# Decode kernel (grouped-query attention mixed with a gated MLP): the output row summed in two halves on two column groups, the final copy on two engines

## The chip, the cores and the metric

The kernel runs on one core of one Trainium2 chip. The metric is the device time of one execution in microseconds.

## The reference

One token is decoded. `g` is a scalar gate, `a` attention over a cache of 65,536 positions with 16 query heads and 8 key/value heads of size 256, `b` a small gated MLP, and the result is one row of 448 numbers.

```python
def reference(A_x, A_k_cache, A_v_cache, A_wq, A_wo, B_x, B_W_gate, B_W_up, B_W_down, gate_w):
    g = sigmoid((A_x * gate_w).sum(-1))
    q = (x @ wq) as 16 heads of 256
    o = softmax(q k^T / 16) v          # k, v: [8 heads, 65536, 256] bf16, 256 MiB each
    a = o @ wo                         # 4096 -> 448
    h = max(x @ W_gate, 0) * (x @ W_up)
    b = h @ W_down                     # 1792 -> 448
    return g * a + (1 - g) * b
```

## The kernel before

K and V come in tiles of 8 MiB through a ring of three buffers. Each K tile is transposed on VectorE and multiplied on TensorE; each V tile is multiplied on TensorE. The gates are folded in earlier, so that the MLP's down projection (`f_dn`) and the attention's output projection (`f_wo`) can add into one bank of PSUM (the memory that the matmul engine writes its sums to), `A_ps`. Both have a single output row: the weight operand is one column of 128 values, and the moving operand is a 128x448 block. A column group below is the part of the matmul array that `tile_position=(0, 32 * g)` selects in the code; its output row lies in PSUM partition 32 * g.

```python
# the MLP's weights live in ring buffer 2, which the third K tile will overwrite
wd_sb = ring[2][:, 0:FT * D].rearrange("p (ft d) -> p ft d", ft=FT)
slot, held, freed = {}, {2: ["gu", "dn"]}, {}      # K tile 2 waits for gate/up and for the down projection
...
def f_dn(e):                                       # 14 matmuls, one column group
    for ft in range(FT):
        ins = e.matmul(A_ps[0:1, 0:D], hT[:, ft:ft + 1], wd_sb[:, ft, :], start=(ft == 0), stop=False, ...)
...
def f_wo(e, ...):                                  # 32 matmuls, s=0 in partition 0, s=1 in partition 32
    for j in range(lo, hi):
        for s in range(2):
            r_ = 32 if s == 1 and j < J - 1 else 0     # the very last j: both in partition 0
            ins = e.matmul(A_ps[r_:r_ + 1, 0:D], attnT[:, c:c + 1], wo_sb[:, j, s, :], ..., tile_position=(0, r_))
...
if i == 3:                                         # partition 32 is copied out while the last two matmuls run
    f0 = op("ac", ..., lambda e: e.copy(a_sb, A_ps[32:33, 0:D]), ...)
f1 = op("dv", T_END, lambda e: e.tensor_tensor(fin_o, A_ps[0:1, 0:D], a_sb, ALU.add), [fin, f0])
f2 = dma("sp", T_END + 1, "out", lambda e: e.dma_start(out[0, :, :], fin_o), [f1])
```

Of the kernel before, what the change touches and what calls it, by code (L numbers as in the profile page):

```python
# [7 lines left out]
F32 = mybir.dt.float32  # L8
# [4 lines left out]
ALU = AluOpType  # L13
# [11 lines left out]
class _Plan:  # L25
# [8 lines left out]
    def op(self, eng, key, fn, deps=()):  # L34
        o = _Op(eng, key, fn, deps)
        self.ops.append(o)
        return o

    def dma(self, eng, key, sem, fn, deps=()):
        if sem not in self.dsem:  # L40
            self.dsem[sem] = self.es.enter_context(self.nc.semaphore("d_" + sem))
        o = _Op(eng, key, fn, deps, dma=sem)
        self.ops.append(o)
        return o
# [46 lines left out]
def bass_gated_mix__gqa_block_cached__glu_gated_reglu__decode_kernel(  # L91
# [13 lines left out]
    H = A_k_cache.shape[1]  # L105
    S = A_k_cache.shape[2]
    DH = A_k_cache.shape[3]
    D = A_x.shape[2]
    F = B_W_gate.shape[1]
    NQ = A_wq.shape[1]  # L110
    J = 2 * H
# [15 lines left out]
    with es:  # L127
# [5 lines left out]
        ptp = [sb("ptp%d" % i, [128, 1024], BF) for i in range(2)]  # L133
# [18 lines left out]
        attnT = sb("attnT", [128, H * 4], BF)  # L152
        hT = sb("hT", [128, FT], BF)
# [7 lines left out]
        fin_o = P_sb[0:1, 0:D]  # L161
        gw_row = ptp[1][0:1, 0:D]
        xeo = ptp[1][0:1, 448:704]
        qrep = ptp[1][:, 704:960]
        a_sb = ptp[H % 2][0:1, 0:2 * D].bitcast(F32)
        gtmp = ptp[0][0:1, 0:2 * D].bitcast(F32)

        wq3 = ring[2][:, 0:R3 * NQ]
# [6 lines left out]
        wd_sb = ring[2][:, 0:FT * D].rearrange("p (ft d) -> p ft d", ft=FT)  # L175
# [4 lines left out]
        A_ps = ps("A_ps", [128, 512], F32)  # L180
# [11 lines left out]
        op, dma = pl.op, pl.dma  # L192
# [31 lines left out]
        T_END = t + 20.0  # L224
# [9 lines left out]
        wo_sb = ring[slot["wo", 0]][:, 0:J * 2 * D].rearrange("p (j s n) -> p j s n", j=J, s=2)  # L234
# [103 lines left out]
        def f_qk(n, b, sl):  # L338
# [12 lines left out]
                return ins  # L351
            return f

        l_, qk, smax, aexp, pv, last = {}, {}, {}, {}, {}, {}
        pending = []

# [40 lines left out]
        for kind, i, t in issue:  # L397
# [34 lines left out]
            elif kind == "wd":  # L432
                a3 = dma("sp", t, "wd", lambda e: e.dma_start(wd_sb, B_W_down.rearrange("(p ft) d -> p ft d", ft=FT)), [l_["q"]])

                def f_dn(e):
                    for ft in range(FT):
                        ins = e.matmul(A_ps[0:1, 0:D], hT[:, ft:ft + 1], wd_sb[:, ft, :], start=(ft == 0), stop=False,
                                       skip_group_check=True)
                    return ins
                l_["dn"] = op("pe", max(tg + 12.2, tL["wd", 0]), f_dn, [l_["hT"], a3])  # L440
            elif kind == "k":
                n = i
# [13 lines left out]
                if t_ == NTH - 1:  # L456
# [12 lines left out]
                    ev = []  # L469
# [53 lines left out]
                l_["wo", i] = dma("sp", t, "wo%d" % i, lambda e, lo=lo, hi=hi: e.dma_start(  # L523
                    wo_sb[:, lo:hi, :, :], A_wo[lo * 256:hi * 256, :].rearrange("(j p s) n -> p j s n", p=128, s=2)), free(("wo", 0)))


        LAST = last["tn", H - 1]
        for i, (lo, hi) in enumerate(WO):
            for h in range(lo // 2, (hi + 1) // 2):
                key = max(tL["wo", i], last["tn", h] + 0.5) + 0.01 * h  # L530
                if i in (1, 2):
                    key = LAST - (0.7, 0.2)[i - 1]
                elif i > 2:
                    key = LAST + 2 + 0.1 * i

                def f_wo(e, h=h, lo=max(lo, 2 * h), hi=min(hi, 2 * h + 2)):
                    for j in range(lo, hi):
                        for s in range(2):
                            c = h * 4 + s * 2 + j - 2 * h
                            r_ = 32 if s == 1 and j < J - 1 else 0  # L540
                            ins = e.matmul(A_ps[r_:r_ + 1, 0:D], attnT[:, c:c + 1], wo_sb[:, j, s, :],  # L541
                                           start=(s == 1 and j == 0), stop=(j == J - 1 or (j == J - 2 and s == 1)),
                                           skip_group_check=True, tile_position=(0, r_))
                    return ins
                fin = op("pe", key, f_wo, [l_["wo", i], last["norm", h], l_["dn"]])
                if i == 3:
                    f0 = op("ac", key + 0.01, lambda e: e.copy(a_sb, A_ps[32:33, 0:D]), [fin, last["ev", H - 2][1]])
        f1 = op("dv", T_END, lambda e: e.tensor_tensor(fin_o, A_ps[0:1, 0:D], a_sb, ALU.add), [fin, f0])
        f2 = dma("sp", T_END + 1, "out", lambda e: e.dma_start(out[0, :, :], fin_o), [f1])

        pl.serialize(touch_m)
        progs = pl.finish()
# [53 lines left out]
```

## Time and profile before

| | before |
|---|---|
| median of the first three runs | 1284.96 us (1284.89 to 1285.78) |
| span of the profiled run | 1284.6 us |
| busy: PE, DVE, ACT | 33%, 49%, 5% |
| read from HBM | 549.03 MB, 427 GB/s over the span |

In the profiles PE is TensorE, the matmul engine, and PEld its weight loads; DVE is VectorE, ACT ScalarE, POOL GpSimd, and SPq the queue from which SyncE issues loads. These lines are from the page of the kernel before: the first gives busy time of each engine, the second the busy share of the 16 DMA engines in tenths for 40 slices of the span.

```profile
PE 425.8 (33%) x4554; PEld 159.9 (12%) x4554; DVE 633.8 (49%) x421; ACT 61.6 (5%) x116; POOL 4.1 (0%) x21
...
DMA  9999999999999999999999999999999999999997
...
DMA packets 12974, 549.65 MB, mean 428 GB/s; under 512 B 1283, under 2 KB 3590, under 8 KB 3974
```

No compute engine is near full, and the DMA row is full everywhere but in the last slice: the body waits for memory. Work on an engine can then cost time in only two ways: it can hold back the issue of a load until the DMA engines run dry, or it can lie behind the last load. Both exist here. First, part of the chain of work that ended last (start us, length us, what):

```profile
53.14 5.08 PE ST L348 x54
58.23 2.61 PE A_ps L437 x14
...
60.85 0.33 SPq L445
...
61.23 43.56 DMA ring<-in_A_k_cache_dram
```

L437 is the down projection. When its 14 matmuls are done, the SP queue issues the third K tile (L445). Second, the end of the kernel, from its timeline (start us, length us, engine, line, operation, output<-input, shape, count, and in brackets the idle time before):

```profile
1278.73 0.69 DVE L381 CAST o_sb<-O 128x512 bf16<-128x512 f32 x1 [55.80 <-PE O L370]
...
1279.21 0.91 PE L541 MATMUL A_ps<-ring,attnT 128*1 128x448 bf16 x4 [0.54 <-DMA ring<-in_A_wo_dram]
...
1280.35 2.04 PE L541 MATMUL A_ps<-ring,attnT 128*1 128x448 bf16 x8
1280.36 0.16 DVE L390 TENSOR_TENSOR attnT<-M_ps,hs 128x4 bf16<-128x4 f32 x1 [0.94 <-PE M_ps L386]
...
1281.67 0.52 ACT L547 COPY ptp<-A_ps 1x448 f32<-1x448 f32 x1 [58.86 <-PE A_ps L541]
1282.43 0.61 DVE L548 TENSOR_TENSOR P_sb<-A_ps,ptp 1x448 bf16<-1x448 f32 x1 [1.91 <-PE A_ps L541]
1283.07 0.32 SPq L549 DMA_DIRECT2D out_dram<-P_sb  x1
```

The matmuls at 1279.21 start when the last big piece of output weights has landed. From there to the output's issue it takes 1283.07 - 1279.21 = 3.86 us. I call this "the end" below; it is a chain without gaps to hide in. The last eight matmuls take 2.04 us, and one VectorE addition of 0.61 us stands alone behind them.

### The profile page before, as it was taken

How to read it: one execution, taken by the hardware profiler on the slowest of the kernel's cores; microseconds unless marked ns; L12 is line 12 of the kernel's file. 1: busy time of each engine (PE TensorE's matmuls, PEld its weight loads, DVE VectorE, ACT ScalarE, POOL GpSimd, SP SyncE). 2: the span in 40 equal slices, each digit the busy share in tenths (PEclk: the TensorE clock that was granted, in tenths of full speed). 3: DMA queues.
4: the chain of work that ended last, by engine and by line, in shares of the span. 5: the costliest groups of instructions: out<-in, count | busy, mean ns of one | idle time of the engine just before them, and what ended most of it. 6: DMA issues, size and time to landing. Idle time of an engine off the chain costs nothing.

```text
span 1284.6 us, 9827 instructions
## 1 busy us (share of the span) xinstructions
PE 425.8 (33%) x4554; PEld 159.9 (12%) x4554; DVE 633.8 (49%) x421; ACT 61.6 (5%) x116; POOL 4.1 (0%) x21
## 2 busy tenths in 40 slices
PE   3624322334123431224331343331333323233235
PEld 2401100111001110001110111110111101011011
DVE  2588633465433655434555444555434556335600
ACT  0000000000000000000000000000000000000000
POOL 1000000000000000000000000000000000000000
PEclk8656666656566565666655666655666656666676
DMA  9999999999999999999999999999999999999997
GB/s 398 420 425 447 429 429 439 431 429 435 439 427 432 430 437 435 427 437 437 429 427 437 437 427 433 433 433 429 445 429 425 435 435 431 433 435 429 437 397 315
DMA packets 12974, 549.65 MB, mean 428 GB/s; under 512 B 1283, under 2 KB 3590, under 8 KB 3974
## 3 DMA queue, kind: packets, MB, share of 16 engines
q1 hardware_dynamic: 12930, 549.03, 99.2%
q8 instruction: 35, 0.57, 0.2%
q14 instruction: 5, 0.04, 0.0%
q10 hardware_dynamic: 4, 0.00, 0.0%
HBM read 549.03 MB, written 0.00 MB: 427 GB/s over the span
## 4 chain that ended last, share of the span: by engine, by line
DVE 34%; DMA 32%; another core or an unknown queue 16%; PE 15%; SPq 1%; ACT 1%; issue 1%
DVE ring L336 30%; DMA ring<-in_A_k_cache_dram 27%; PE ST L348 7%; PE O L370 6%; DMA ring<-in_B_W_up_dram 3%; DMA ring<-in_A_wo_dram 2%; DVE P_sb L473 1%; SPq L514 1%; DVE nmb L451 1%; PE PT L478 1%; PE M_ps L421 1%; PE M_ps L424 0%; ACT ptp L487 0%; DVE o_sb L381 0%
## 5 line engine op out<-in xcount | busy, mean ns | idle before, releaser
L336 DVE STREAM_TRANSPOSE ring<-ring 128x2048 uint32<-128x2048 uint32 x256 | 565.4, 2275 | 413.1 <-DMA ring<-in_A_k_cache_dram 413.1
L348 PE MATMUL ST<-ring,xm 128*16 128x512 bf16 x2048 | 224.7, 613 | 759.0 <-DVE ring L336 759.0
L348 PEld LDWEIGHTS ST<-ring,xm 128*16 128x16 bf16 x2048 | 61.6, 120 | 908.1 <-DVE ring L336 799.4
L370 PE MATMUL O<-ring,ptp 128*4 128x512 bf16 x2048 | 146.2, 447 | 34.5 <-DMA ring<-in_A_v_cache_dram 30.4
L453 ACT ACTIVATE P_sb<-ST,nmb 128x512 bf16<-128x512 f32 x32 | 45.2, 1411 | 1115.8 <-DVE nmb L451 1115.8
L451 DVE TENSOR_REDUCE nmb<-ST 128x1 f32<-128x512 f32 x32 | 22.1, 689 | 110.4 <-PE ST L348 110.4
L370 PEld LDWEIGHTS O<-ring,ptp 128*4 128x4 bf16 x2048 | 53.9, 98 | 126.6 <-issue 54.3
L381 DVE CAST o_sb<-O 128x512 bf16<-128x512 f32 x8 | 5.5, 692 | 79.3 <-PE O L370 79.3
L473 DVE TENSOR_TENSOR P_sb<-P_sb,hs 128x1024 bf16<-128x1024 bf16 x16 | 18.9, 1222 | 8.3 <-ACT hs L467 8.3
L478 PE MATMUL PT<-identb,P_sb 128*128 128x128 bf16 x128 | 16.5, 311 | 15.5 <-DVE P_sb L473 14.7
L421 PE MATMUL M_ps<-xT,ring 128*128 128x1 bf16 x84 | 9.5, 205 | 16.3 <-DMA ring<-in_B_W_up_dram 16.3
L478 PEld LDWEIGHTS PT<-identb,P_sb 128*128 128x128 bf16 x128 | 12.3, 141 | 18.3 <-DVE P_sb L473 18.3
L487 ACT COPY ptp<-PT 128x256 bf16<-128x256 bf16 x32 | 10.3, 375 | 23.0 <-PE PT L478 23.0
L308 PE MATMUL M_ps<-ring,P_sb 128*128 128x256 bf16 x64 | 10.0, 334 | 3.2 <-DMA ring<-in_A_wq_dram 3.2
L421 PEld LDWEIGHTS M_ps<-xT,ring 128*128 128x128 bf16 x84 | 7.2, 152 | 16.9 <-issue 16.5
L453 ACT ACTIVATION_READ_ACCUMULATOR P_sb<-ST,nmb 128x1 f32 x32 | 8.4, 262 | 0.0
L308 PEld LDWEIGHTS M_ps<-ring,P_sb 128*128 128x128 bf16 x64 | 7.5, 119 | 5.5 <-issue 3.2
L424 PE MATMUL M_ps<-xT,ring 128*64 128x1 bf16 x56 | 7.8, 276 | 0.0
L404 DVE STREAM_TRANSPOSE ptp<-P_sb 128x128 uint32<-128x128 uint32 x1 | 0.3, 312 | 13.4 <-ACT P_sb L403 13.4
L463 PE MATMUL M_ps<-identf,hs 128*2 128x128 f32 x8 | 2.4, 296 | 10.0 <-DVE hs L461 10.0
L424 PEld LDWEIGHTS M_ps<-xT,ring 128*64 128x64 bf16 x56 | 5.4, 191 | 0.4
L541 PE MATMUL A_ps<-ring,attnT 128*1 128x448 bf16 x32 | 5.0, 430 | 0.6 <-DMA ring<-in_A_wo_dram 0.5
(72 smaller groups left out, 59.4 us busy)
## 6 DMA issues: line engine op xcount, KB each, us to landing
ring<-in_A_v_cache_dram SPq DMA_DIRECT2D x1, 4096.0 KB, 29.6
ring<-in_A_wq_dram SPq DMA_DIRECT2D x1, 3072.0 KB, 10.4
ring<-in_A_wo_dram SPq DMA_DIRECT2D x1, 2240.0 KB, 30.1
ring<-in_A_v_cache_dram SPq DMA_DIRECT2D x1, 2048.0 KB, 22.9
ring<-in_B_W_down_dram SPq DMA_DIRECT2D x1, 1568.0 KB, 20.7
ring<-in_B_W_gate_dram SPq DMA_DIRECT2D x1, 1344.0 KB, 32.8
ring<-in_B_W_up_dram SPq DMA_DIRECT2D x1, 1344.0 KB, 35.4
ring<-in_A_v_cache_dram SPq DMA_DIRECT2D x1, 1024.0 KB, 24.9
```

The costliest lines, as they stand in the source:

```text
L308: ins = e.matmul(QN_ps, xw3[:, k_, 31 - j:159 - j], rhs, start=(j == 0 and kt == 0), stop=(j == J - 1 and kt == R3))
L336: return lambda e: e.transpose(v, v)
L348: ins = e.matmul(bank[32 * w:32 * w + 16, :], xm[:, x0:x0 + 16], ktv[sl][:, u0:u0 + 16, c, :, r_], start=(b == 0 and c == 0 and r_ == 0), ...
L370: ins = e.matmul(OP[h % 2][32 * g:32 * g + 4, :], ptp[h % 2][:, col:col + 13:4], ring[sl][:, k * 512:(k + 1) * 512], start=(a == 0 and k < ...
L421: e.matmul(GU_ps[:, c:c + 1], wf3[which][:, kt * F + ft:(kt + 1) * F:FT], xT[:, kt:kt + 1], start=(kt == 0), stop=False, skip_group_check= ...
L424: ins = e.matmul(GU_ps[64 * half:64 * half + 64, c:c + 1], wfh[which][:, ft:F // 2:FT], xT[:, R3 + half:R3 + half + 1], start=False, stop= ...
L451: smax[n] = op("dv", tk + 22, lambda e, n=n, NM=NM, t_=t_: e.tensor_reduce(NM[:, t_:t_ + 1], ST[n % 2][:], AX.X, ALU.max, negate=True), [q ...
L453: aexp[n] = op("ac", tk + 23, lambda e, n=n, t_=t_, NM=NM, RS=RS: e.activation(P_sb[:, t_:2048:4], ST[n % 2][:], ACTF.Exp, bias=NM[:, t_:t ...
L473: rsc = op("dv", tt, lambda e, X=X, pb=pb: e.tensor_tensor(pb, pb, X[:, 12:16].unsqueeze(1).to_broadcast([128, 256, 4]), ALU.mult), [h7, a ...
L478: ins = e.transpose(PT[rd][:, s * 128:(s + 1) * 128], P_sb[:, (rd * 8 + s) * 128:(rd * 8 + s + 1) * 128], identb[:, :])
L487: ins = e.copy(dst, src)
L514: dep = dma("sp", t, "vp%d" % i, lambda e, sl=sl, n=n, lo=lo, hi=hi: e.dma_start(ring[sl][:, lo * 256:hi * 256], v_src(n)[:, lo * 256:hi * ...
```

## The change

Each projection matmul of 448 columns becomes two of 224 on two column groups (partition 0 and partition 32). The halves need no addition at the end; VectorE copies one and ScalarE the other.

```diff
+        D2 = D // 2
+        def proj(e, lhsT, rhs, start, stop):
+            for g in range(2):
+                ins = e.matmul(A_ps[32 * g:32 * g + 1, 0:D2], lhsT, rhs[:, g * D2:(g + 1) * D2], start=start, stop=stop,
+                               skip_group_check=True, tile_position=(0, 32 * g))
+            return ins
...
-                        ins = e.matmul(A_ps[0:1, 0:D], hT[:, ft:ft + 1], wd_sb[:, ft, :], start=(ft == 0), stop=False,
-                                       skip_group_check=True)
+                        ins = proj(e, hT[:, ft:ft + 1], wd_sb[:, ft, :], ft == 0, False)
...
-                            r_ = 32 if s == 1 and j < J - 1 else 0
-                            ins = e.matmul(A_ps[r_:r_ + 1, 0:D], attnT[:, c:c + 1], wo_sb[:, j, s, :],
-                                           start=(s == 1 and j == 0), stop=(j == J - 1 or (j == J - 2 and s == 1)),
-                                           skip_group_check=True, tile_position=(0, r_))
+                            ins = proj(e, attnT[:, c:c + 1], wo_sb[:, j, s, :], False, j == J - 1 and s == 1)
...
-                if i == 3:
-                    f0 = op("ac", key + 0.01, lambda e: e.copy(a_sb, A_ps[32:33, 0:D]), [fin, last["ev", H - 2][1]])
-        f1 = op("dv", T_END, lambda e: e.tensor_tensor(fin_o, A_ps[0:1, 0:D], a_sb, ALU.add), [fin, f0])
-        f2 = dma("sp", T_END + 1, "out", lambda e: e.dma_start(out[0, :, :], fin_o), [f1])
+        f0 = op("dv", T_END, lambda e: e.tensor_copy(fin_o[:, 0:D2], A_ps[0:1, 0:D2]), [fin])
+        f1 = op("ac", T_END, lambda e: e.copy(fin_o[:, D2:D], A_ps[32:33, 0:D2]), [fin])
+        f2 = dma("sp", T_END + 1, "out", lambda e: e.dma_start(out[0, :, :], fin_o), [f0, f1])
```

More of the change, by code (lines that the diff above doesn't have):

```diff
@@ L164, in bass_gated_mix__gqa_block_cached__glu_gated_reglu__decode_kernel @@
         qrep = ptp[1][:, 704:960]
-        a_sb = ptp[H % 2][0:1, 0:2 * D].bitcast(F32)
         gtmp = ptp[0][0:1, 0:2 * D].bitcast(F32)
```

## The prediction

> **What bounds the kernel now.** The page shows 549.65 MB moved at 428 GB/s, the DMA row in its top tenth in every slice but the last. The Trainium skill, "DMA: Bandwidth & Descriptors", section "Where 436 GB/s comes from", gives a fabric ceiling of 435 GB/s[...]. PE is busy 33%, DVE 49%, ACT 5%. So the body is bound by the stream from HBM; engine time counts only where it delays a load's issue while the queue runs dry, and behind the last load.
>
> **What the change touches.** Only 46 matmuls of 448 columns (14 in the down projection, L437, and 32 in the output projection, L541) and the last two copies. Each matmul becomes two of 224 columns on two column groups.
>
> **1. Down projection, on the issue path of a K tile.** The waits of the SP queue show one K load waiting 37.5 us for L437, and the chain of waits shows L437 at 58.23 us for 2.61 us, then the K issue at 60.85. The 14 matmuls run one after another in one column group, 0.19 us apart at full clock. The packet records show that around 61 to 63 us about 12 of 16 DMA engines stand empty, on average 0.66 us per engine, before the packets of this load start. As 14 pairs of 224 columns on two groups, the work should need about 14 x 0.09 us = 1.3 to 1.6 us (estimate; the score matmuls of L348 run at 53 ns each on four groups, so issuing keeps up). The K load is then issued about 1.1 us earlier and the gap mostly closes. A few engines did not idle there, so I count 0.3 to 0.7 us of it, say 0.4.
>
> **2. Output projection, behind the last load.** The first 20 matmuls (1258.6 us) lie under loads. The last 12 run at half clock (windows view: 0.50). They were already paired on two groups, except the last two, which run one after the other. The final eight take 2.04 us: five steps of about 0.37 us. After: eight steps of about 0.19 us, so about 0.35 us less. If issuing twice as many pairs binds, only 0.1 us. The Trainium skill, "TensorEngine Tiling (Array Packing)", section "Key Properties", says tiles load weights and multiply in parallel; L370's 64 matmuls on four groups agree (83 ns each where one shows 447 ns).
>
> **3. Final copy.** The DVE addition of 1x448 takes 0.612 us at the very end; the ACT copy (0.523 us) was hidden. Now DVE and ACT each copy 224 elements in parallel: estimate 0.38 us DVE (128x512 cast took 0.69), 0.36 us ACT. Saves 0.2 us.
>
> **Sum.** 0.4 + 0.3 + 0.2 = 0.9 us, 0.07% of the time. Predicted 1284.0 us; range 1281.8 to 1285.8. Chances: faster by over 2%: 0.01; within 2%: 0.98; slower by over 2%: 0.01.
>
> **What would show each step.** (1) L437's group: 28 matmuls, span near 1.4 us; the K issue near 59.8 us; the empty stretch near 61 us smaller. (2) 64 matmuls in the output projection; from the last attention scaling on DVE to the final copy about 1.5 us instead of 1.9. (3) Two copies of about 0.37 us side by side. DMA volume and rate unchanged.
>
> **What would make it wrong.** The DMA engines that never idled set the pace, so step 1 gives nothing; the halves serialize in one group (down projection stays 2.6 us); a switch of tile layout between the transposes and the projection costs more than before; or runs differ by more than the effect (three runs before spread 0.9 us).

## The result, and the profile after

The changed kernel took 1285.04 us (median of four runs, 1284.70 to 1285.65), beside 1285.37 us for the kernel before (four runs, 1284.89 to 1286.22). The ratio is 0.9997, with a 95% interval of 0.998 to 1.0015. By these runs alone nothing can be told apart from zero.

The traces say more. The same part of the chain in the changed kernel, where the down projection is L358:

```profile
52.92 5.17 PE ST L347 x54
58.09 1.34 PE A_ps L358 x27
...
59.44 0.33 SPq L452
...
59.81 43.62 DMA ring<-in_A_k_cache_dram
```

The down projection went from 2.61 to 1.34 us in the chain, and the K tile was issued at 59.44 instead of 60.85 us. The end, from the timeline of the changed kernel:

```profile
1277.46 0.69 DVE L389 CAST o_sb<-O 128x512 bf16<-128x512 f32 x1 [57.09 <-PE O L378]
...
1278.50 0.91 PE L358 MATMUL A_ps<-ring,attnT 128*1 128x224 bf16 x8 [1.08 <-DMA ring<-in_A_wo_dram]
...
1279.61 1.66 PE L358 MATMUL A_ps<-ring,attnT 128*1 128x224 bf16 x16
1279.64 0.16 DVE L398 TENSOR_TENSOR attnT<-M_ps,hs 128x4 bf16<-128x4 f32 x1 [1.48 <-PE M_ps L394]
...
1281.31 0.34 ACT L550 CAST P_sb<-A_ps 1x224 bf16<-1x224 f32 x1 [61.04 <-PE A_ps L358]
1281.31 0.38 DVE L549 CAST P_sb<-A_ps 1x224 bf16<-1x224 f32 x1 [1.51 <-PE A_ps L358]
1281.73 0.32 SPq L551 DMA_DIRECT2D out_dram<-P_sb  x1
```

The end now takes 1281.73 - 1278.50 = 3.23 us, 0.63 less: the last matmuls 1.66 instead of 2.04 us (sixteen halves in eight steps, where there were five whole steps), and the last copy 0.38 instead of 0.61 us. The page of the changed kernel shows the same stream: 428 GB/s and a full DMA row. The profiled spans differ by 1.3 us (1284.6 and 1283.3), almost four times what the means of the runs differ by (0.35 us). Part of this is the draw: the profiled execution of the kernel before took 1286.37 us, longer than all of its four timed runs. So the question was which number is the change's, and what makes the other.

### The profile page after: what moved, and what is told of

Its sections match the earlier page's. It is cut to its first block, busy times and chain, and to the rows that moved or that the text cites. A ratio compares the mean times of both kernels' runs of the same rounds, so it can differ in the third digit from the quotient of the medians.

```text
span 1283.3 us, 9919 instructions
## 1 busy us (share of the span) xinstructions
PE 427.0 (33%) x4600; PEld 162.9 (13%) x4600; DVE 633.6 (49%) x421; ACT 61.5 (5%) x116; POOL 4.1 (0%) x21
## 4 chain that ended last, share of the span: by engine, by line
DVE 34%; DMA 32%; another core or an unknown queue 16%; PE 15%; SPq 1%; ACT 1%; issue 1%
DVE ring L335 30%; DMA ring<-in_A_k_cache_dram 27%; PE ST L347 7%; PE O L378 6%; DMA ring<-in_B_W_up_dram 3%; DMA ring<-in_A_wo_dram 2%; DVE P_sb L480 1%; SPq L521 1%; DVE nmb L458 1%; PE PT L485 1%; PE M_ps L429 1%; PE M_ps L432 0%; ACT ptp L494 0%; DVE o_sb L389 0%
## 5 line engine op out<-in xcount | busy, mean ns | idle before, releaser
L378 PE MATMUL O<-ring,ptp 128*4 128x512 bf16 x2048 | 149.0, 453 | 34.3 <-DMA ring<-in_A_v_cache_dram 30.3
L358 PE MATMUL A_ps<-ring,attnT 128*1 128x224 bf16 x64 | 4.6, 305 | 2.5 <-DMA ring<-in_A_wo_dram 2.5
```

The lines of the kernel that those rows point to most:

```text
L378: ins = e.matmul(OP[h % 2][32 * g:32 * g + 4, :], ptp[h % 2][:, col:col + 13:4], ring[sl][:, k * 512:(k + 1) * 512], start=(a == 0 and k < ...
```

## The experiments

My theory: the change saves at two places, by an earlier K issue (because the DMA engines run dry before it) and by a shorter end. Rival A: an earlier K issue gives nothing, because a few DMA engines never idled there. Rival B: the gain is given back elsewhere.

Each experiment was timed in rounds beside the kernel before on the same chip. The table gives mean times; the difference is to the mean of before (nine runs each, means of 1285.99 to 1286.23 us). r1 to r4 share nine runs of before, r5 to r8 another, r9 to r11 a third; r12 has its own.

| run | what | runs | mean us | less than before | lowest to highest |
|---|---|---|---|---|---|
| r1_after_again | the change | 5 | 1285.04 | 1.15 | 1284.69 to 1285.64 |
| r2_dn_pair | down projection only | 5 | 1285.70 | 0.49 | 1284.46 to 1286.43 |
| r3_tail_only | end only | 5 | 1285.67 | 0.52 | 1284.98 to 1286.47 |
| r4_early_dn | before, down projection earlier in order | 5 | 1285.48 | 0.71 | 1284.16 to 1286.35 |
| r5_before_dn5 | before, down projection five times | 4 | 1296.87 | -10.85 | 1296.65 to 1297.33 |
| r6_after_dn5 | the change, down projection five times | 4 | 1289.97 | -3.95 | 1289.14 to 1290.43 |
| r7_one_copier | the change, VectorE copies both halves | 5 | 1284.74 | 1.28 | 1283.86 to 1285.59 |
| r8_four | four column groups | 5 | 1285.29 | 0.73 | 1284.28 to 1286.37 |
| r9_split_before | before, K load cut in two | 5 | 1284.07 | 1.92 | 1283.82 to 1284.37 |
| r10_split_after | the change, K load cut in two | 5 | 1283.30 | 2.69 | 1283.23 to 1283.34 |
| r11_split_four | four groups, K load cut in two | 5 | 1283.81 | 2.17 | 1283.47 to 1284.04 |
| r12_split_one | r10, VectorE copies both halves | 5 | 1283.94 | 2.29 | 1283.58 to 1284.38 |

The second table is from the traces, one per run. "Lost" is worked out from the DMA packet records between 58 and 75 us: the time that engines stood without a packet (counted as the packets in flight that were missing to 16) plus the time by which 64 KB packets took longer than their usual 2.42 us, both summed and divided by 16 engines. "Weights landed" is the start of the first projection matmuls of the end, which wait for the output weights. Where the load was cut, "K tile issued" is its first piece.

| trace | matmul clock rises, us | down projection starts, us | its matmuls take, us | K tile issued, us | lost, us | weights landed, us | the end, us |
|---|---|---|---|---|---|---|---|
| before | 55.90 | 58.02 | 2.81 | 60.85 | 1.56 | 1279.21 | 3.86 |
| after | 55.77 | 57.89 | 1.51 | 59.44 | 0.63 | 1278.50 | 3.23 |
| r1_after_again | 58.13 | 59.18 | 1.50 | 60.72 | 1.48 | 1278.72 | 3.27 |
| r2_dn_pair | 57.56 | 58.85 | 1.49 | 60.38 | 1.64 | 1278.24 | 3.85 |
| r3_tail_only | 55.62 | 57.74 | 2.46 | 60.23 | 0.89 | 1278.45 | 3.22 |
| r4_early_dn | 58.38 | 56.09 (weights) | about 4.2 | 60.28 | 1.27 | 1277.74 | 3.84 |
| r5_before_dn5 | 57.87 | 58.94 | 13.40 | 72.38 | 12.43 | 1289.49 | 3.85 |
| r6_after_dn5 | 57.16 | 58.43 | 6.88 | 65.34 | 5.50 | 1282.56 | 3.27 |
| r7_one_copier | 55.45 | 57.68 | 1.55 | 59.26 | 0.06 | 1276.86 | 3.66 |
| r8_four | 57.03 | 58.56 | 0.90 | 59.49 | 0.97 | 1277.42 | 2.98 |
| r9_split_before | 57.20 | 58.78 | 2.81 | 53.33 | 0.04 | 1276.52 | 3.84 |
| r10_split_after | 56.22 | 58.09 | 1.54 | 53.00 | 0.04 | 1276.75 | 3.26 |
| r11_split_four | 58.02 | 58.98 | 0.86 | 53.08 | 0.04 | 1277.07 | 2.98 |
| r12_split_one | 56.24 | 58.13 | 1.52 | 53.04 | 0.04 | 1277.03 | 3.65 |

### r1_after_again: the change once more

No edit.

> The changed kernel once more, with more rounds. My theory (0.4 us from the earlier K issue, 0.6 us from the shorter end) expects 0.6 to 1.2 us less than before, a ratio near 0.9993. Rival A (the earlier K issue gives nothing, since a few DMA engines never idled) expects 0.4 to 0.6 us less. Rival B (all of it is given back, as the end of the stream moves by more than that) expects 0 +- 0.2 us. In the trace: end of the last projection matmul group to the end of the final copy as in the first profile (final copy 0.38 us).

It was 1.15 us faster than before (ratio 0.999, interval 0.9976 to 1.0004), within what my theory expected but not clear of zero. Its trace holds the surprise: the same kernel as in the first profile issued the K tile 1.28 us later, at 60.72 us, nearly as late as the kernel before. The score matmuls and the K issue, from the timeline of the first trace of the changed kernel:

```profile
52.85 5.24 PE L347 MATMUL ST<-ring,xm 128*16 128x512 bf16 x64
...
59.44 0.80 SPq L452 DMA_DIRECT2D ring<-in_A_k_cache_dram  x2
```

The same in r1_after_again:

```profile
53.25 6.11 PE L347 MATMUL ST<-ring,xm 128*16 128x512 bf16 x64
...
60.72 0.80 SPq L452 DMA_DIRECT2D ring<-in_A_k_cache_dram  x2
```

These are the busy times by microsecond in the first trace of the changed kernel (window, its length, busy us and count of PE, PEld, DVE, ACT, POOL, granted matmul clock, DMA share, GB/s):

```profile
55.00:56.00 1.00, 1.00 (x16) 0.32 (x12) 0.00 (x0) 0.00 (x0) 0.00 (x0) 0.62 0.15 66
56.00:57.00 1.00, 1.00 (x24) 0.47 (x20) 0.00 (x0) 0.00 (x0) 0.00 (x0) 1.00 1.88 803
57.00:58.00 1.00, 1.00 (x24) 0.48 (x18) 0.00 (x0) 0.00 (x0) 0.00 (x0) 1.00 0.63 262
```

And these are the same windows in r1_after_again:

```profile
55.00:56.00 1.00, 1.00 (x16) 0.34 (x12) 0.00 (x0) 0.00 (x0) 0.00 (x0) 0.50 0.15 66
...
57.00:58.00 1.00, 1.00 (x16) 0.36 (x12) 0.00 (x0) 0.00 (x0) 0.00 (x0) 0.50 0.64 262
58.00:59.00 1.00, 1.00 (x24) 0.41 (x18) 0.00 (x0) 0.00 (x0) 0.00 (x0) 0.94 1.12 467
```

In the first trace the matmul clock went from half to full speed within the microsecond from 55 us, in the second only in the one from 58 us. The score matmuls ahead of the down projection end 1.27 us later: they started 0.40 us later, and at the slower clock they took 0.87 us longer. The Trainium skill, "TensorE: Matmul & The Clock Gate", section "What's actually happening", says that the clock is set by a free-running activity window of 3413 ns, so that the moment of the change depends on where the window happens to lie. The traces agree with the window: the clock records change at distances of 3.41, 6.83, 10.24 us and so on, all whole multiples of 3.41. For the size of the variation the section gives ±500 ns; here the rise falls anywhere between 55.45 and 58.38 us (second table), 2.65 to 5.24 us after the score matmuls began, and this measured range decides. The one-column matmuls before them did not raise the clock: from 40 to 50 us in the trace of before PE was busy for all 10 us, at half clock. So the K issue carries a delay that differs from run to run by about as much as the change saves there.

### r2_dn_pair: only the down projection on two groups

```diff
-                        ins = e.matmul(A_ps[0:1, 0:D], hT[:, ft:ft + 1], wd_sb[:, ft, :], start=(ft == 0), stop=False, ...)
+                        r_ = 32 * (ft % 2)
+                        ins = e.matmul(A_ps[r_:r_ + 1, 0:D], hT[:, ft:ft + 1], wd_sb[:, ft, :], start=(ft < 2), stop=False,
+                                       ..., tile_position=(0, r_))
```

> The kernel before with only the down projection spread over two column groups: even terms in one, odd terms in the other, still 448 columns each, the end unchanged. My theory: the 14 matmuls take about 1.4 us instead of 2.6, the K issue after them comes 1.1 to 1.4 us earlier, and the whole is 0.3 to 0.7 us faster than before. Rival A: the K issue is earlier too, but the time is unchanged (within 0.2 us).

The 14 matmuls took 1.49 us instead of 2.81, so what helps is that two groups work at once, whether each gets half of the columns or half of the terms. The run was 0.49 us faster on average (interval of the ratio 0.9983 to 1.0008), in line with the theory but, with runs 2 us apart, not proof. What was left out of the diff: `f_wo` no longer starts the sum of partition 32, which the down projection now does. In its one trace the clock rose at 57.56 us, and the K issue was only 0.47 us earlier than in the trace of before.

### r3_tail_only: the halves of the down projection one group after the other

```diff
-                    for ft in range(FT):
-                        ins = proj(e, hT[:, ft:ft + 1], wd_sb[:, ft, :], ft == 0, False)
+                    for g in range(2):
+                        for ft in range(FT):
+                            ins = e.matmul(A_ps[32 * g:32 * g + 1, 0:D2], hT[:, ft:ft + 1],
+                                           wd_sb[:, ft, g * D2:(g + 1) * D2], start=(ft == 0), stop=False, ...)
```

> The changed kernel with the halves of the down projection issued one column group after the other: 14 matmuls of 224 columns in the first, then 14 in the second. My theory: they no longer overlap, so the 28 take about 2.6 us (14 x 2 x 0.093) or more, the K issue is back near 60.8 us, and only the end is shorter: 0.5 to 0.7 us faster than before by the trace of the end. Rival: if halving the width alone were what helps, the 28 would take about 1.5 us.

The 28 halves took 2.46 us in this order and 1.51 us interleaved. Narrower matmuls alone save little (2.81 to 2.46 us); the order that keeps both groups busy saves the rest. The run was 0.52 us faster than before on average (interval of the ratio 0.9983 to 1.0008), and its end took 3.22 us, as in the changed kernel.

### r4_early_dn: the down projection moved ahead

```diff
-                l_["relu"] = mop("dv", tg + 12, ...)
+                l_["relu"] = mop("dv", tg + 8, ...)
-                l_["hT"] = mop("dv", tg + 12.1, ...)
+                l_["hT"] = mop("dv", tg + 8.1, ...)
-                l_["dn"] = op("pe", max(tg + 12.2, tL["wd", 0]), f_dn, [l_["hT"], a3])
+                l_["dn"] = op("pe", tg + 8.2, f_dn, [l_["hT"], a3])
```

> The kernel before with nothing but the order changed on the matmul engine: the down projection goes between the two halves of the first tile's score matmuls rather than behind them. The K issue that waits for it should come near 57.3 us, 3.5 us earlier, so the empty stretch of the DMA engines near 61 us vanishes altogether. My theory: 0.5 to 0.7 us faster than before, all of the 0.66 us gap. Rival A (engines that never idled set the pace): unchanged within 0.2 us. A cost could come back: the second half of the scores is 2.6 us later.

This missed. The projection did start about 2 us earlier, at 56.09 us, but there it ran at half clock, and the K issue came at 60.28 us, not 57.3. These are weight loads of it and the K issue, from the timeline:

```profile
56.52 0.12 PEld L437 LDWEIGHTS A_ps<-ring,hT 128*1 128x1 bf16 x1 [0.30 <-issue]
56.89 0.13 PEld L437 LDWEIGHTS A_ps<-ring,hT 128*1 128x1 bf16 x1 [0.24 <-issue]
57.26 0.13 PEld L437 LDWEIGHTS A_ps<-ring,hT 128*1 128x1 bf16 x1 [0.24 <-issue]
...
60.28 2.10 SPq L445 DMA_DIRECT2D ring<-in_A_k_cache_dram  x2
```

They come 0.37 us apart, twice the 0.19 us of the full clock. The move put the serial matmuls into the cold stretch; a reordering that is right by count can be wrong by clock. The 0.71 us by which its runs were faster (interval of the ratio 0.9981 to 1.0006) can't be told from zero.

### r5_before_dn5 and r6_after_dn5: the down projection five times

```diff
-                    for ft in range(FT):
+                    for ft in list(range(FT)) * 5:
```

> The kernel before with the down projection done five times over (each pass starts the sum anew, so the result stays right). The K issue comes 4 x 2.61 = 10.4 us later. My theory: the queue is empty by then, so nearly every microsecond is paid: 9 to 10.5 us slower than before. Rival A (other engines or later slack absorb a late K issue): under 5 us slower.

> The changed kernel with the down projection done five times over. Each pass of 28 half-width matmuls on two groups costs about 1.3 us, so the K issue comes 5.2 to 5.6 us later than in the changed kernel. My theory: 4 to 5.6 us slower than before, so 5 us less than the same fivefold in the kernel before. If the halves did not overlap, both fivefold kernels would be equally slow.

Here the effect is far above the noise: the intervals of both ratios (1.0084, from 1.007 to 1.0098, and 1.003, from 1.0017 to 1.0044) lie clear of 1. Four added passes cost the kernel before 10.85 us, 2.71 each; a pass of it is 14 x 0.19 = 2.6 us long. Four passes cost the changed kernel 3.95 + 1.15 = 5.1 us (taking r1, on another chip, as its time without them), 1.3 each. The two timelines show the passes (140 and 70 matmuls) and the K issue. First the kernel before with five passes:

```profile
58.94 13.40 PE L437 MATMUL A_ps<-ring,hT 128*1 128x448 bf16 x70
...
72.38 0.80 SPq L445 DMA_DIRECT2D ring<-in_A_k_cache_dram  x2
```

Then the changed kernel with five passes:

```profile
58.43 6.88 PE L358 MATMUL A_ps<-ring,hT 128*1 128x224 bf16 x140
...
65.34 0.80 SPq L452 DMA_DIRECT2D ring<-in_A_k_cache_dram  x2
```

From one to the other the K issue moved by 7.04 us and the landing of the weights at the far end by 6.93 us (1289.49 - 1282.56). A late K issue is paid one for one, 1200 us later: Rival A falls, at least where the queue has run dry. The Trainium skill, "TensorEngine Tiling (Array Packing)", section "Key Properties", says that different tiles load weights and multiply in parallel; here 140 half-width matmuls took 6.88 us and 70 full ones 13.40 us, which agrees.

### r7_one_copier: ScalarE left out

```diff
-        f1 = op("ac", T_END, lambda e: e.copy(fin_o[:, D2:D], A_ps[32:33, 0:D2]), [fin])
+        f1 = op("dv", T_END + 0.01, lambda e: e.tensor_copy(fin_o[:, D2:D], A_ps[32:33, 0:D2]), [fin])
```

> The changed kernel with both final copies on VectorE, one after the other, ScalarE left out. The second copy starts after the first: about 0.38 us more at the end of the chain, so between the last matmul and the output's issue 0.8 us instead of 0.42. The time should be 0.3 to 0.5 us above the changed kernel's. Rival: waiting for one engine rather than two makes up for it, difference under 0.1 us.

By time it came out level with the change or better, on another chip than r1 (1.28 us below before, where the change was 1.15 below), against my expectation. By its trace the end took 3.66 us, 0.4 us more than with two copiers, exactly as expected; but the clock rose early (55.45 us), nothing was lost at the K issue (0.06 us), and the weights landed 1.6 us earlier than in the first trace of the changed kernel. The trace is of the fastest of the five runs. The part that differs from run to run was larger than the effect and can have hidden it. This is why the kernels r9 to r11 were made.

### r8_four: four column groups

```diff
-            for g in range(2):
-                ins = e.matmul(A_ps[32 * g:32 * g + 1, 0:D2], lhsT, rhs[:, g * D2:(g + 1) * D2], ...)
+            for g in range(4):
+                ins = e.matmul(A_ps[32 * g:32 * g + 1, 0:D4], lhsT, rhs[:, g * D4:(g + 1) * D4], ...)
...
+        f0 = op("dv", T_END, lambda e: e.tensor_copy(fin_o, A_ps[:, 0:D4]), [fin])       # 128 x 112
+        f2 = dma("sp", T_END + 1, "out", lambda e: e.dma_start(out[0, 0, :].rearrange("(g n) -> g n", g=4), fin_o[0:128:32, :]), [f0])
```

`A_ps` is also cleared at the start, since all its partitions are copied.

> The change taken one step on: four column groups of 112 columns, one VectorE copy of 128 partitions by 112 for all of them, output written from partitions 0, 32, 64 and 96. If columns still bind, the down projection takes about 0.7 to 0.9 us[...] and the final 32 matmuls about 1.0 us instead of 1.68; the copy 0.26 us. Then 0.6 to 1.2 us below the changed kernel. If the issue of twice as many weight loads and matmuls binds[...], both projections take as long as with two groups or longer, and only the copy's 0.1 us is won.

Columns still bind in the down projection: 56 matmuls of 112 columns took 0.90 us. The end took 2.98 us, another 0.3 less, but it is no longer a chain of engine work alone: by the chain that ended last, its last eight matmuls waited for the last piece of output weights, which landed at 1279.65 us (in r11 they waited in the same way). But the output is now written from four partitions, and the time was not better than with two groups. The last three lines of its timeline:

```profile
1279.69 0.35 PE L358 MATMUL A_ps<-ring,attnT 128*1 128x112 bf16 x8 [0.20 <-DMA ring<-in_A_wo_dram]
1280.10 0.28 DVE L549 CAST P_sb<-A_ps 128x112 bf16<-128x112 f32 x1 [1.73 <-PE A_ps L358]
1280.40 0.65 SPq L550 DMA_DIRECT2D out_dram<-P_sb  x1
```

The issue takes 0.65 us instead of 0.32, and from its start to the end of the span it is 1282.5 - 1280.40 = 2.1 us, where the changed kernel's single row takes 1283.3 - 1281.73 = 1.6 us. By the traces, the 0.5 us lost there is more than the 0.3 us won at the end.

### r9_split_before, r10_split_after, r11_split_four: the K load freed from the down projection

The down projection's weights occupy 19% of ring buffer 2. The third K tile's load is cut into a large piece that doesn't touch them and a small one that does.

```diff
+                if n == 2:
+                    dma("sp", t, "r%d" % sl, lambda e, n=n, sl=sl: e.dma_start(ring[sl][:, FT * D:], k_src(n)[:, FT * D:]), [l_["gu"]])
+                c1 = FT * D if n == 2 else U * DH
-                kd = dma("sp", t, "r%d" % sl, lambda e, n=n, sl=sl: e.dma_start(ring[sl][:], k_src(n)), free(("k", n)))
+                kd = dma("sp", t + 0.01, "r%d" % sl, lambda e, n=n, sl=sl, c1=c1: e.dma_start(ring[sl][:, 0:c1], k_src(n)[:, 0:c1]), free(("k", n)))
```

> The kernel before, with the third K tile's load cut in two: the 81% of the buffer that the down projection's weights don't occupy is loaded as soon as the gate and up projections are done (near 53 us), the rest after the down projection. The first part of the load no longer waits for the down projection, so neither its length nor the moment at which the matmul clock rises should matter. My theory: no empty stretch near 61 us, the last V cast on VectorE near 1276.4 us as in the fastest trace so far, and 1.5 to 2.5 us faster than before. Rival (the stream's end is set elsewhere, its agreement with the K issue is chance): within 0.7 us of before.

> The same cut of the load in the changed kernel. With the queue's start out of play, only the end is left of the change: 0.6 us (from the last V cast to the output's issue 3.75 instead of 4.34 us) below the cut kernel of before, and 2 to 3 us below the kernel before. If the change's gain were in the start alone, the two cut kernels would be equal.

> The cut load with four column groups of 112 columns. The end was 3.46 us with four groups, so 0.3 us below the cut changed kernel, 0.9 us below the cut kernel of before, 2.3 to 3.3 us below the kernel before; the fastest so far.

The large piece is issued near 53 us in all three, nothing is lost at the DMA engines near 61 us, and the weights land at 1276.5 to 1277.1 us, earlier than in every trace without the cut but that of r7, where almost nothing was lost there either. r9 was 1.92 us faster than before (ratio 0.9984, interval 0.9972 to 0.9997): the kernel before plus this cut beats the changed kernel (their ranges, 1283.82 to 1284.37 and 1284.69 to 1285.65 us, don't meet, but the chips differ). Not all of the 1.92 us need come from the K issue. By the packet records, every uncut kernel with a single down projection also had a second dry stretch, near 1250 us, of 0.10 to 0.75 us per engine (0.75 in the trace of before); r9 to r12 had none. Why the cut removes it too isn't shown. And the runs close up: the five runs of r10 lie within 0.11 us, where the nine of before lie within 2.55 us (1285.10 to 1287.65). So the cut removed most of the scatter of before (r9's five runs lie within 0.55 us); which of the two dry stretches made it isn't separated.

On this quiet base the change can be weighed: r10 lies 1284.07 - 1283.30 = 0.77 us below r9. The ranges (1283.23 to 1283.34, and 1283.82 to 1284.37) don't meet. The end explains 0.58 us of it (3.84 and 3.26 us); the rest is within the spread of r9. For the end this answers Rival B: the gain isn't given back. The ends side by side, from the chain of work that ended last, first r9:

```profile
1276.52 0.91 PE A_ps L544 x4
1277.43 0.20 PE M_ps L386 x4
...
1277.65 2.05 PE A_ps L544 x7
...
1279.72 0.61 DVE P_sb L551
```

then r10:

```profile
1276.75 0.91 PE A_ps L358 x4
1277.65 0.20 PE M_ps L394 x4
...
1277.88 1.68 PE A_ps L358 x16
...
1279.58 0.38 DVE P_sb L552
```

The first projection step (0.91 us) and the transposes (0.20 us) are alike; the last step and the copy are 0.37 and 0.23 us shorter. r11, which I had expected to be fastest, was 0.51 us slower than r10: the end was 0.28 us shorter as foreseen, but I had left the dearer output write out of the sum although r8 showed it. The write costs about 0.56 us more (from its issue to the end of the span 2.05 us in r11, 1.49 us in r10), so the two together explain about 0.3 of the 0.51 us. r10 is the fastest version, 0.21% below the kernel before (ratio 0.9978, interval 0.9965 to 0.9992).

### r12_split_one: the copy's share on the quiet base

The edit of r7 on r10.

> The changed kernel with the cut load, and with both final copies on VectorE one after the other. On this base runs agree within 0.1 us, so the share of the split copy can be read: 0.4 us above the cut changed kernel (one more VectorE copy of 0.38 us behind the first), 1283.7 us, so still 0.3 us below the cut kernel of before. Rival: waiting for one engine rather than two gives it back, 1283.3 us.

It lost 0.40 us of r10's lead over before (2.29 us instead of 2.69, on another chip, each against its own runs of before). That difference has a standard error of about 0.4 us (estimated from the scatter of the runs), so the time alone proves nothing; the trace does. Its end took 3.65 us instead of 3.26, by a second copy of 0.38 us behind the first:

```profile
1279.86 0.38 DVE L552 CAST P_sb<-A_ps 1x224 bf16<-1x224 f32 x1 [1.52 <-PE A_ps L358]
1280.27 0.38 DVE L553 CAST P_sb<-A_ps 1x224 bf16<-1x224 f32 x1
1280.68 0.32 SPq L554 DMA_DIRECT2D out_dram<-P_sb  x1
```

The Trainium skill, "TensorEngine Tiling (Array Packing)", section "PSUM Bottleneck", advises to use both ScalarE and VectorE for taking data out of PSUM; for this row of 448 it was worth 0.39 us of the end. Without it the halves would save only 3.84 - 3.65 = 0.2 us there, since two VectorE copies of 224 (0.38 us each) cost more than the one addition of 448 (0.61 us) that they replace.

## Why the prediction was right or wrong

The prediction was right: 1285.04 us lies inside its range of 1281.8 to 1285.8 us. That alone tests nothing, since the kernel before, at 1285.37 us, lies inside it too; the steps have to be looked at one by one:

- **What bounds the kernel: right.** r5, r6 and r9 show that work ahead of a late load issue sets the time, and r9 against r10 that work at the end does. Engine work elsewhere was not tested.
- **Step 1, the earlier K issue, 0.4 us: right in mechanism, the size rests on chance that I did not see.** The down projection shrank from 2.81 to 1.51 us as estimated (1.3 to 1.6), and with a dry queue that is paid one for one (r5, r6), so up to 1.3 us is at stake, not a part of the 0.66 us of empty engines. That gap was not all: the first packets after it were also slow, another 0.90 us per engine in the trace of before. Nor did the gap "mostly close" every time: from 0.66 us it went to 0.27 us in the first trace of the changed kernel, but to 0.59 us in r1. What a run gets of it depends on when the matmul clock rises, which moved over 2.9 us between traces. r2 alone gave 0.49 us on average, near the 0.4, with an interval that includes zero.
- **Step 2, the last matmuls, 0.35 us: right.** The last step went from 2.04 to 1.66 us. Issue of twice as many instructions did not bind; r8's down projection shows that even four groups don't reach that limit.
- **Step 3, the final copy, 0.2 us: right.** From 0.61 to 0.38 us (VectorE, predicted 0.38) beside 0.34 us (ScalarE, predicted 0.36). r12 shows that the second engine is what makes this step positive.
- **The sum, 0.9 us, and the level, 1284.0 us.** The first four runs showed 0.3 us, five more 1.15 us; each has an interval that includes zero. Weighted by their scatter, the two together give about 0.8 us, with a 95% interval of about 0.2 to 1.3 us (an estimate). That the predicted 0.9 us lies near its middle is partly luck (step 1). The level was 1 us too low: 0.4 us because its base was (1284.96 us, where the four runs beside the change had 1285.37), 0.6 us because the gain in these four runs was smaller. Three runs were too few for a base: the 40 runs of before have a mean of 1286.04 and a standard deviation of 0.74 us. I listed run-to-run scatter as a danger but took no account of where in it three runs may lie.

What stays open: the weights' landing is not fully explained by what was lost at the K issue (in the trace of after 0.63 us were lost and the weights landed at 1278.50 us, in that of r4 1.27 us were lost and they landed at 1277.74). Most of this goes away when the second dry stretch near 1250 us is added: in all 2.31 us were lost in the trace of before, 2.00 in r1, 1.37 in r4, 1.12 in r8 and 0.04 in r9 to r12, and the weights landed in that order. The trace of after (0.91 us) still falls out, because there the weights came 1.69 us behind the start of the last V matmuls, where the others show 1.1 to 1.2 us (r3, which falls out a little, 1.43 us); the cause isn't known. The second stretch was 0.10 to 0.75 us in the uncut kernels with one down projection and absent with five passes and with the cut; no experiment was made for it. And why r9, r11 and r12 scatter by 0.5 to 0.8 us but r10 by 0.1 us is not known; with five runs each it may be chance.

## What to carry to other kernels

In a kernel bound by its loads, look for work that gates the issue of a load while the queue is about to run dry: there a microsecond of work cost a microsecond of time (r5, r6), and cutting the load so that most of it doesn't wait (r9, 1.9 us) was, by the means, worth more than making the work faster (r2, 0.5 us, not clear of zero). This single-row projection took 2.81 us on one column group, 1.51 us on two and 0.90 us on four, but count what the split costs at its other end: a second copy, or an output written from several partitions. Where the effect is smaller than the scatter, find and remove the source of the scatter, or multiply the suspected piece (r5, r6), before adding rounds.

## What the Trainium skill lacked or had wrong

- "TensorE: Matmul & The Clock Gate", section "Wait — 56ns, not 53.3ns?", says that start-to-start of matmuls never drops below about 25 ns however small they are. Taken for matmuls on different column groups, that sentence doesn't hold. In r8, 56 matmuls of 112 columns on four column groups took 0.90 us in all, the last one's 0.21 us of latency included, so (0.90 - 0.21) / 55 = 13 ns from start to start, weight loads between them; the K load that waits for all of them was issued 0.93 us after the first one's start. Within one group that is about 50 ns, so for a single group r8 doesn't test it.
- The same page, section "What's actually happening", gives ±500 ns for how far the clock's rise varies. Here it moved over 2.9 us between traces. The page lacks that this can move a load's issue: with the later rise the score matmuls took 0.87 us longer and the K load behind them went out later. Where most of that load was taken off the matmuls' path, five runs lay within 0.11 to 0.57 us (r9 to r11), where the nine runs of before lay within 2.55 us.
- "DMA: Bandwidth & Descriptors" gives sizes at which transfers are efficient. What I did not find there is that the packets after a dry stretch are slow too: the trace of before had 0.66 us of empty engines at a late issue, and the 64 KB packets after it took a further 0.90 us per engine longer than their usual 2.42 us, which was as large a loss as the gap.
- The same page: 896 bytes written from four partitions instead of one took 0.65 us instead of 0.32 us to issue, and 0.5 us longer from issue to the end of the span (r8); I found no figure for this.
